# A convolution and a low-rank mixer on one core: two h clusters a slot in place of three, and the conv at other pieces of W2

## The chip, the cores and the metric

The kernel runs on one core of a Trainium2 chip. The metric is the time of one execution on the device in microseconds (us): the median of 3 runs was 324.3 us (324.24 to 325.69). One further execution was profiled. It took 324.34 us, and the span from its first to its last instruction was 322.4 us. All times below are in us unless another unit stands there.

## The reference

The input `x` has 8 batches of 4224 rows (positions) with 192 columns. A causal convolution of 7 taps, with softmax weights for each of 8 heads of 24 columns, gives `y`. Then a mixer adds a low-rank product along the positions, and a two-layer network along the columns:

```python
y   = lightweight_conv(x, softmax(weight))        # 7 taps back, 8 heads of 24 columns
tt  = U.T @ y                                     # per batch: 32 x 192, the "sums"
u   = y + V.T @ tt                                # the second term is "h"
out = u + relu(u @ w_ch1) @ w_ch2                 # 192 -> 768 -> 192
```

The output is float32, 8 x 4224 x 192.

## The kernel before, in words

Positions are cut into tiles of 128: 33 tiles a batch (`NT`), 264 in all, and 33 groups of 8 tiles (`NG`, `GT`) that run across the borders of the batches. Tiles are counted through, so batch b has tiles 33b to 33b + 32, and group g has 8g to 8g + 7.

The steps of the work, and the engine of each:

- **conv** (`conv32`, lines 331 to 363): for two or three heads, 8 small matmuls a head (L349, 64 rows by 32 columns of the array) fill two banks of PSUM, and each bank is copied to `y_sb` by ScalarE ("A") or VectorE ("D"), as a pattern such as `AAD` says, taken in turn. Half of the matmuls read `xb_sb`, a shifted copy of `x_sb` that GpSimd makes (`x_shift`, lines 296 to 327).
- **sums** (`tt_mm`, `tt_split`, `tt_sum`): 33 matmuls (L412) make U.T y in four column groups; ScalarE takes `tt_hi` (L426), VectorE takes `tt_lo` (L427); later two matmuls (L438) add the four groups up, and VectorE writes `tt_sb` (L432). h needs `tt_sb` of its batch.
- **h** (`h_tiles`, lines 458 to 498): a matmul for each tile (L469, 32 rows of the array, so that four row groups can run at once; row group = pair number modulo 4). Two tiles of a batch, an even one and the next, share a PSUM bank. In a call, all even tiles are issued, and then all odd ones. VectorE adds `y_sb` and writes `u_sb` (L492), one add for a bank, or two where the bank's two tiles lie in different halves of four tiles.
- **transposes** (`transp`): a DMA on SP's queue turns a group's `u_sb` into `uT`.
- **W1** (`w1`): 36 matmuls a group (L587, 64 rows by 128 columns, two at once); relu to `rl_sb` on ScalarE (L601) or VectorE (L603), 7 and 5 a group.
- **W2** (`w2`): two tiles are a piece, with 12 matmuls on the whole array (L614), one bank, an add on VectorE (L623) and a transfer to the output on SP's queue.

All matmul results pass through one pool of eight PSUM banks, which are given out in turn (`bank()`); a bank is handed on when its last reader has finished.

The order is written by hand. A list `SLOTS` (lines 650 to 702) has for each slot the groups whose W1 runs first, the groups whose W2 then runs piece by piece, and a table `at`: before piece p of the slot, do these other steps. From slot 5 on a slot has three groups, so 12 pieces. Names in the table: `c5:0:2:A` is conv of batch 5, from head 0, two heads, copies on ScalarE; `x6:4` four of the six shifting steps of batch 6; `t5` and `s5` the two halves of the sums; `h16` is h of group 16 with its transpose. Slots 6 to 9 do conv and sums of batches 4 to 7 beside W2; slots 10 to 13 have no conv left. Loads of `x` are issued on GpSimd's queue during W1 (`LOADS`, `x_load`), and two of the six shifting steps go between them. Pools with few buffers: `xs` 2, `xbs` 1, `ys` 3, `us` 7, `uts` 5.

Of the kernel before, what the change touches and what calls it, by code (L numbers as in the profile page):

```python
# [14 lines left out]
def kernel(  # L15
# [12 lines left out]
    B, S, D = x.shape  # L28
# [7 lines left out]
    GT = 8  # L36
    NTT = B * NT
    NG = NTT // GT
# [292 lines left out]
    def conv32(b, h0, nh, engs):  # L331


        if yt[b] is None:
            yt[b] = ys.tile([P, NT, D], BF16, name="y_sb")
        nk = (NB0 // 2, NB1 // 2)
        for n in range(nh):
            h = h0 + n
            hs = slice(h * GS, h * GS + GS)
            pp = [bank(), bank()]  # L340
            for cg in range(4):
                t, w, st = (
                    (xt[b], bands[h // HQ][:, h % HQ, QB : 2 * QB], 1 + cg // 2)
                    if cg % 2
                    else (xbt[b], band2[:, h, :], cg // 2)
                )
                for r in range(2):
                    hr = slice(HB * r, HB * r + HB)
                    nc.tensor.matmul(  # L349
                        out=pp[r][QB * cg : QB * cg + QB, 0 : nk[r] * GS],  # L350
                        lhsT=w[hr],
                        rhs=t[hr, st : st + 2 * nk[r] - 1 : 2, hs],
                        start=True,
                        stop=True,
                        tile_position=(HB * r, QB * cg),
                    )
            for part in range(2):
                j0 = NB0 // 2 * part
                evac(
                    engs[(2 * n + part) % len(engs)],  # L360
                    yt[b][:, j0 : j0 + nk[part], hs],
                    pp[part][:, 0 : nk[part] * GS].rearrange("p (k a) -> p k a", a=GS),
                )
# [42 lines left out]
    def tt_mm(b, js, p=None):  # L406

        if p is None:
            p = bank()
        for n, j in enumerate(js):  # L410
            c = n % 4
            nc.tensor.matmul(  # L412
                out=p[32 * c : 32 * c + 32, 0:D],
                lhsT=U_sb[:, j // 4, j % 4, :],
                rhs=yt[b][:, j, :],
                start=(n < 4),
                stop=(n + 4 >= len(js)),
                tile_position=(0, 32 * c),
            )
        return p  # L420

    def tt_split(b, p):

        hi = sml.tile([P, D], BF16, name="tt_hi")
        lo = sml.tile([P, D], BF16, name="tt_lo")
        nc.scalar.activation(out=hi[:], in_=p[:, 0:D], func=ACT.Copy)  # L426
        nc.vector.tensor_tensor(out=lo[:], in0=p[:, 0:D], in1=hi[:], op=ALU.subtract)  # L427
        ttb[b] += [hi, lo]
# [29 lines left out]
    def h_tiles(b, j0, j1):  # L458

        banks = {}  # L460
        for a in range(2):
            for pr in range(j0 // 2, (j1 + 1) // 2):
                j = 2 * pr + a
                if not j0 <= j < j1:
                    continue
                q = pr % 4
                if pr not in banks:
                    banks[pr] = bank()
                last = nc.tensor.matmul(  # L469
                    out=banks[pr][:, a * D : (a + 1) * D],  # L470
                    lhsT=V_sb[32 * q : 32 * q + 32, (j // 8) * 2 + j % 2, :],
                    rhs=ttb[b][32 * q : 32 * q + 32, :],
                    start=True,
                    stop=True,
                    tile_position=(32 * q, 0),
                )
        done.append(last)
        for pr in sorted(banks):
            js = [j for j in (2 * pr, 2 * pr + 1) if j0 <= j < j1]
            runs = []  # L480
            for j in js:
                t = b * NT + j
                if runs and t % 4 != 0:
                    runs[-1].append(j)
                else:
                    runs.append([j])
            for run in runs:
                n = len(run)
                t = b * NT + run[0]
                g, hf, i = t // GT, (t % GT) // 4, t % 4  # L490
                a = run[0] % 2
                nc.vector.tensor_tensor(  # L492
                    out=u_group(g)[:, i : i + n, :, hf, :],
                    in0=yt[b][:, run[0] : run[0] + n, :].rearrange("p n (c k) -> p n c k", c=3),
                    in1=banks[pr][:, a * D : (a + n) * D].rearrange(
                        "p (n c k) -> p n c k", n=n, c=3
                    ),
                    op=ALU.add,
                )

    def h_group(g):
        t0, t1 = g * GT, g * GT + GT
        while t0 < t1:
            b = t0 // NT
            te = min(t1, (b + 1) * NT)
            h_tiles(b, t0 - b * NT, te - b * NT)
            t0 = te

    def transp(g):
        uTt[g] = uts.tile([P, 4, 3, P], BF16, name="uT")  # L510
        return nc.sync.dma_start_transpose(
            out=uTt[g][:].rearrange("p i c t -> p (i c) t"),
            in_=ut[g][:].rearrange("p i c f k -> p (i c f k)"),
        )
# [118 lines left out]
    def held(ins, after):  # L633
        tc.add_manual_dep(
            ins.ins,
            after.ins.name,
            mybir.DependencyInfo(mybir.DependencyClass.Sync, mybir.DependencyReason.DATA),
            reason="transfer held back",
        )

    def x_load(b, q, after):
        if q == 0:
            x_tile(b)
            x_zero(b, nc.gpsimd)
        held(x_part(b, *XP[q]), after)
# [4 lines left out]
    SLOTS = [  # L650
        ([0], [], {}),
        ([1], [0], {0: ["h0", "l2:0", "l2:1"], 1: ["h3", "l2:2"]}),
        (
            [2],
            [1],
            {0: ["d1", "x2:1", "l2:3", "x2:5", "h1"], 1: ["t1"], 3: ["s1"], 4: ["h4"]},
        ),
        ([3], [2], {1: ["h5"], 3: ["h6"]}),
# [12 lines left out]
            },  # L671
        ),
    ]
    nh = 10
    for k in range(5, 14):
        gs = list(range(3 * k - 9, 3 * k - 6))
        hs = [f"h{g}" for g in range(nh, min(nh + 3, NG))] + [None] * 3
        nh = min(nh + 3, NG)
        if k == 5:
            at = {  # L680
                2: ["c3:0:3:AAD"],
                3: ["c3:3:3:AAD"],
                4: ["c3:6:2:A", "x4:4"],
                5: [hs[0]],
                6: ["t3"],
                8: ["s3", hs[1]],
                11: [hs[2]],
            }
        elif k < 10:
            b = k - 2  # L690
            at = {
                0: [f"c{b}:0:2:A"],
                2: [f"c{b}:2:3:AAD"],
                3: [f"c{b}:5:3:AAD"] + ([f"x{b + 1}:4"] if b + 1 < B else []),
                5: [f"t{b}", hs[0]],
                7: [f"s{b}"],
                8: [hs[1]],
                11: [hs[2]],
            }
        else:  # L700
            at = {0: [hs[0]], 4: [hs[1]], 8: [hs[2]]}
        SLOTS.append((gs, gs, {p: [w for w in what if w] for p, what in at.items()}))
    assert nh == NG

    LOADS = {3: [(4, 1), (4, 4), (5, 1), (5, 4)]}
    for b in range(4, B):
        g = 3 * b - 6
# [83 lines left out]
    def do(what):  # L791
        if what[0] == "c":
            b, h0, n, engs = what[1:].split(":")
            conv32(int(b), int(h0), int(n), engs)
            return
        if what[0] == "d":
            for h in range(H):
                last = conv(int(what[1:]), h, 1, [0, 1], "AA" if h == 2 else "AD")
            held(transp(3), last)
            done.append(last)  # L800
            return
        if what[0] == "l":
            b, q = (int(v) for v in what[1:].split(":"))
            x_load(b, q, done[-1])
            return
        if what[0] == "x":
            b, n = (int(v) for v in what[1:].split(":"))
            if not steps:
                steps.extend(x_shift(b))
            for _ in range(n):  # L810
                steps.pop(0)()
            return
        n = int(what[1:])
        if what[0] == "h":
            h_group(n)
            if n > 1 and n != 3:
                transp(n)
        elif what[0] == "t":
            tt_split(n, tt_mm(n, range(NT)))
        else:  # L820
            tt_sum(n)

    for gs1, gs2, at in SLOTS:
# [13 lines left out]
        for p in range(npc + 1):  # L837
            for what in at.get(p, []):
                do(what)
            if p < npc:  # L840
                g, k = gs2[p // 4], p % 4
# [35 lines left out]
```

## Time and profile before

| quantity | value |
|---|---|
| median of 3 runs | 324.3 us |
| profiled execution: time, span | 324.34 us, 322.4 us |
| granted TensorE clock | 1.00 |
| TensorE busy with matmuls | 316.4 us, 98% |
| VectorE, ScalarE, GpSimd busy | 268.9, 169.6, 141.8 us |
| W2 (L614) | 1584 matmuls |
| W1 (L587) | 1188 matmuls |
| h (L469) | 264 matmuls, 168 adds on VectorE (L492) |
| conv (L349), from batch 2 on | 384 matmuls |

How to read it: the profile's page has busy times, a chain that ended last (followed back from the last instruction), and groups of instructions. The same chain can be shown in order of time, as pieces "start, duration, engine and line, how many instructions". A timeline of one engine has for each run of instructions the start, the duration, the operation, out<-in with shapes, and in brackets the idle time ahead of it and what ended it. Matmuls are pipelined: a row's duration is longer than the distance to the next row, so what a matmul costs is read from starts. The same holds for VectorE: durations overlap by some 0.08 us.

### The profile page before, as it was taken

Reading aid. Unit: us, or ns where it says so; the run is one execution under the profiler, and the core shown is the slowest. Engines: PE = TensorE matmul, PEld = TensorE weight load, DVE = VectorE, ACT = ScalarE, POOL = GpSimd, SP = SyncE. Lnnn points to the kernel's source line nnn. Section 1 sums busy time; section 2 is a strip of 40 time slices with the busy share of each in tenths; the row PEclk is TensorE's granted clock in tenths of the full one; section 3 lists DMA queues with packets and bytes.
Section 4 is the critical chain, followed back from the end, with each engine's and each line's share of the span. In section 5 each row is a group of like instructions: output and inputs, shape, how many; then the busy total and the mean of one; then the engine's idle time right before and its main releaser. Section 6 shows DMA issues by size and latency. Waiting matters only on the chain.

```text
span 322.4 us, 9590 instructions
## 1 busy us (share of the span) xinstructions
PE 316.4 (98%) x4004; PEld 223.3 (69%) x4004; DVE 268.9 (83%) x550; ACT 169.6 (53%) x344; POOL 141.8 (44%) x108
## 2 busy tenths in 40 slices
PE   8999999999999999999999999999999999999996
PEld 3757576478678647867864884687797497487495
DVE  6769989987977986997898699789888897896864
ACT  1766723960874397088249609824903902912910
POOL 8763299429937983992897497000000000000000
PEclk9999999999999999999999999999999999999999
DMA  8999994999997999799689966138269059039035
GB/s 103 191 195 169 200 226 104 213 179 243 190 188 142 266 151 191 151 185 190 170 230 187 188 171 173 51 107 232 59 177 264 3 148 292 5 97 291 7 121 174
DMA packets 122442, 53.38 MB, mean 166 GB/s; under 512 B 87712, under 2 KB 122400, under 8 KB 122400
## 3 DMA queue, kind: packets, MB, share of 16 engines
q1 hardware_dynamic: 84528, 38.08, 47.4%
q0 software_dynamic: 37728, 14.60, 39.3%
q8 instruction: 31, 0.51, 0.7%
q10 hardware_dynamic: 144, 0.10, 0.1%
q14 instruction: 11, 0.09, 0.1%
HBM read 29.22 MB, written 25.95 MB: 171 GB/s over the span
## 4 chain that ended last, share of the span: by engine, by line
PE 91%; ACT 4%; DMA 2%; DVE 2%; issue 1%; POOL 0%; POOLq 0%
PE ps L614 42%; PE ps L587 39%; PE ps L349 3%; PE ps L469 3%; DMA x_sb<-in_x_dram 2%; PE ps L412 2%; ACT rl_sb L601 2%; ACT y_sb L266 2%; PE ps L379 1%; DVE u_sb L492 1%; DVE rl_sb L603 1%; PE ps L438 0%; PE ps L534 0%; POOL x_sb L79 0%; DVE out_sb L623 0%
## 5 line engine op out<-in xcount | busy, mean ns | idle before, releaser
L601 ACT ACTIVATE rl_sb<-ps 128x512 bf16<-128x512 f32 x233 | 124.3, 604 | 107.7 <-PE ps L587 95.7
L614 PE MATMUL ps<-W_sb,rl_sb 128*128 128x192 bf16 x1584 | 141.2, 246 | 0.2
L614 PEld LDWEIGHTS <-rl_sb 128*128 128x128 bf16 x1584 | 128.3, 98 | 11.8 <-issue 11.4
L587 PE MATMUL ps<-uT,W_sb 64*128 64x512 bf16 x1188 | 131.7, 376 | 0.3 <-DVE uT L268 0.2
L603 DVE TENSOR_SCALAR rl_sb<-ps 128x512 bf16<-128x512 f32 x163 | 105.3, 687 | 14.9 <-PE ps L587 14.7
L587 PEld LDWEIGHTS <-W_sb 64*128 64x128 bf16 x1188 | 66.8, 94 | 60.7 <-issue 4.0
L623 DVE TENSOR_TENSOR out_sb<-ps,u_sb 128x384 f32<-128x384 f32 (+1 forms) x133 | 70.3, 549 | 25.5 <-PE ps L614 25.0
L315 POOL COPY xb_sb<-x_sb 32x3072 bf16<-32x3072 bf16 (+1 forms) x24 | 67.7, 2822 | 1.1
L492 DVE TENSOR_TENSOR u_sb<-y_sb,ps 128x192 bf16<-128x192 bf16 (+1 forms) x168 | 66.2, 460 | 0.0
L303 POOL COPY xb_sb<-x_sb 128x3072 bf16<-128x3072 bf16 x12 | 32.9, 2744 | 39.5 <-PE ps L349 32.4
L266 ACT ACTIVATE y_sb<-ps 128x384 bf16<-128x384 f32 (+4 forms) x90 | 38.3, 519 | 9.8 <-PE ps L349 7.4
L79 POOL DMA_DIRECT2D x_sb<-in_x_dram x32 | 27.1, 853 | 13.9 <-PE ps L469 7.7
L268 DVE CAST y_sb<-ps 128x408 bf16<-128x408 f32 (+4 forms) x36 | 19.1, 577 | 1.4 <-PE ps L379 1.3
L469 PE MATMUL ps<-tt_sb,V_sb 32*128 32x192 bf16 x264 | 12.4, 246 | 0.1
L349 PE MATMUL ps<-x_sb,band 64*32 64x384 bf16 x192 | 12.1, 333 | 0.0
L349 PE MATMUL ps<-xb_sb,band 64*32 64x384 bf16 x192 | 12.1, 332 | 0.0
L469 PEld LDWEIGHTS <-V_sb 32*128 32x128 bf16 x264 | 4.7, 92 | 7.3 <-issue 7.3
L426 ACT ACTIVATE tt_hi<-ps 128x192 bf16<-128x192 f32 x8 | 2.6, 331 | 11.9 <-PE ps L412 11.9
L379 PE MATMUL ps<-x_sb,band 64*64 64x240 bf16 (+3 forms) x192 | 7.9, 275 | 0.5 <-DMA x_sb<-in_x_dram 0.4
L349 PEld LDWEIGHTS <-band 64*32 64x32 bf16 x384 | 4.5, 89 | 5.2 <-issue 2.4
L163 PE MATMUL ps<-zz 128*128 128x512 f32 (+1 forms) x10 | 6.5, 804 | 1.1 <-DVE zz L151 1.1
L379 PEld LDWEIGHTS <-band 64*64 64x64 bf16 x192 | 6.0, 106 | 2.2 <-issue 1.6
(65 smaller groups left out, 67.9 us busy)
## 6 DMA issues: line engine op xcount, KB each, us to landing
out_dram<-out_sb SPq DMA_DIRECT2D x131, 192.0 KB, 2.7
x_sb<-in_x_dram POOLq DMA_DIRECT2D x14, 384.0 KB, 7.6
x_sb<-in_x_dram POOLq DMA_DIRECT2D x7, 432.0 KB, 8.3
x_sb<-in_x_dram POOLq DMA_DIRECT2D x7, 408.0 KB, 7.8
W_sb<-in_moe_w_ch_dram POOLq DMA_DIRECT2D x3, 288.0 KB, 7.5
x_sb<-in_x_dram POOLq DMA_DIRECT2D x1, 504.0 KB, 7.5
uT<-u_sb SPq DMA_TRANSPOSE x31, 4.2
x_sb<-in_x_dram POOLq DMA_DIRECT2D x1, 480.0 KB, 5.7
```

Of the source, the lines that this page charges most:

```text
L79: return nc.gpsimd.dma_start(out=xt[b][HB * r : HB * r + HB, s0:s1, :], in_=x[b, blk * HB : (blk + s1 - s0) * HB, :].rearrange("(j p) d -> ...
L266: nc.scalar.activation(out=out, in_=in_, func=ACT.Copy)
L303: nc.gpsimd.tensor_copy(out=xbt[b][:, s0:s1, :], in_=xt[b][:, s0 + 1 : s1 + 1, :])
L315: nc.gpsimd.tensor_copy(out=xbt[b][q, s0:s1, :], in_=xt[b][q, s0:s1, :])
L349: nc.tensor.matmul(out=pp[r][QB * cg : QB * cg + QB, 0 : nk[r] * GS], lhsT=w[hr], rhs=t[hr, st : st + 2 * nk[r] - 1 : 2, hs], start=True, ...
L469: last = nc.tensor.matmul(out=banks[pr][:, a * D : (a + 1) * D], lhsT=V_sb[32 * q : 32 * q + 32, (j // 8) * 2 + j % 2, :], rhs=ttb[b][32 * ...
L492: nc.vector.tensor_tensor(out=u_group(g)[:, i : i + n, :, hf, :], in0=yt[b][:, run[0] : run[0] + n, :].rearrange("p n (c k) -> p n c k", c=3),
L587: last = nc.tensor.matmul(out=pps[m][hf][:], lhsT=W1_sb[HB * hf : HB * hf + HB, c, m * P : (m + 1) * P], rhs=uTt[g][HB * hf : HB * hf + HB ...
L601: nc.scalar.activation(out=rl[:, m, hf, :], in_=pp[hf][:], func=ACT.Relu)
L603: nc.vector.tensor_scalar_max(out=rl[:, m, hf, :], in0=pp[hf][:], scalar1=0.0)
L614: last = nc.tensor.matmul(out=cps[:, a * D : (a + 1) * D], lhsT=rlt[g][:, m, hf, (i + a) * P : (i + a + 1) * P], rhs=W2_sb[:, m, :], start ...
L623: nc.vector.tensor_tensor(out=o[:, 0:n, :].rearrange("p n (c k) -> p n c k", c=3), in0=cps[:, 0 : n * D].rearrange("p (n c k) -> p n c k", ...
```

## The change

From slot 5 on h is no longer done by groups of 8 tiles but by spans of tiles (`w105:117` and so on): slot 5 has 8, 8 and 9 tiles, slots 6 to 11 have two spans of 11 or 12, slot 12 has 8 and 11. Each span ends at the end of a PSUM bank (an odd tile number within the batch, or the last tile of a batch). After a span, the transposes of all groups that it completes are issued. In slots 6 to 9, conv stands before pieces 0, 2 and 4 in place of 0, 2 and 3, with other patterns of copying engines (`AAD`, `A`, `AD` in place of `A`, `AAD`, `AAD`); h stands before pieces 5 and 9 in place of 5, 8 and 11; the sums begin before piece 9 in place of 5, and end after piece 11 in place of before piece 7. In slots 10 and 11 h stands before pieces 2 and 7, in slot 12 before 0 and 5 (before: 0, 4, 8).

```diff
+    def h_span(t0, t1):
         while t0 < t1:
             b = t0 // NT
             te = min(t1, (b + 1) * NT)
             h_tiles(b, t0 - b * NT, te - b * NT)
             t0 = te
+
+    def h_group(g):
+        h_span(g * GT, g * GT + GT)
...
-    nh = 10
+    spans = {
+        5: [(80, 88), (88, 96), (96, 105)],
+        6: [(105, 117), (117, 129)],
+        7: [(129, 140), (140, 152)],
+        8: [(152, 164), (164, 175)],
+        9: [(175, 187), (187, 198)],
+        10: [(198, 210), (210, 222)],
+        11: [(222, 233), (233, 245)],
+        12: [(245, 253), (253, 264)],
+        13: [],
+    }
     for k in range(5, 14):
         gs = list(range(3 * k - 9, 3 * k - 6))
-        hs = [f"h{g}" for g in range(nh, min(nh + 3, NG))] + [None] * 3
-        nh = min(nh + 3, NG)
+        hs = [f"w{t0}:{t1}" for t0, t1 in spans[k]]
...
         elif k < 10:
             b = k - 2
             at = {
-                0: [f"c{b}:0:2:A"],
-                2: [f"c{b}:2:3:AAD"],
-                3: [f"c{b}:5:3:AAD"] + ([f"x{b + 1}:4"] if b + 1 < B else []),
-                5: [f"t{b}", hs[0]],
-                7: [f"s{b}"],
-                8: [hs[1]],
-                11: [hs[2]],
+                0: [f"c{b}:0:2:AAD"],
+                2: [f"c{b}:2:3:A"],
+                4: [f"c{b}:5:3:AD"] + ([f"x{b + 1}:4"] if b + 1 < B else []),
+                5: [hs[0]],
+                9: [f"t{b}", hs[1]],
+                12: [f"s{b}"],
             }
+        elif k < 13:
+            at = {0 if k == 12 else 2: [hs[0]], 5 if k == 12 else 7: [hs[1]]}
         else:
-            at = {0: [hs[0]], 4: [hs[1]], 8: [hs[2]]}
...
+        if what[0] == "w":
+            t0, t1 = (int(v) for v in what[1:].split(":"))
+            h_span(t0, t1)
+            for g in range(t0 // GT, t1 // GT):
+                transp(g)
+            return
```

More of the change, by code (lines that the diff above doesn't have):

```diff
@@ L499, in h_tiles @@
                 )
-    def h_group(g):
-        t0, t1 = g * GT, g * GT + GT
+    def h_span(t0, t1):
         while t0 < t1:
@@ L691 @@
             at = {
-                0: [f"c{b}:0:2:A"],
-                2: [f"c{b}:2:3:AAD"],
-                3: [f"c{b}:5:3:AAD"] + ([f"x{b + 1}:4"] if b + 1 < B else []),
-                5: [f"t{b}", hs[0]],
-                7: [f"s{b}"],
-                8: [hs[1]],
-                11: [hs[2]],
-            }
-        else:
-            at = {0: [hs[0]], 4: [hs[1]], 8: [hs[2]]}
-        SLOTS.append((gs, gs, {p: [w for w in what if w] for p, what in at.items()}))
-    assert nh == NG
+                0: [f"c{b}:0:2:AAD"],
[4 more added lines that the diff above has]
+                12: [f"s{b}"],
+            }
+        elif k < 13:
+            at = {0 if k == 12 else 2: [hs[0]], 5 if k == 12 else 7: [hs[1]]}
+        else:
+            at = {}
+        SLOTS.append((gs, gs, at))
     LOADS = {3: [(4, 1), (4, 4), (5, 1), (5, 4)]}
```

## The prediction

> **What bounds the kernel now.** I read the page's busy times, then its chain, then the chain in order of time over slots 6 and 7, then VectorE's timeline over the same stretch.
>
> ```profile
> PE 316.4 (98%) x4004; PEld 223.3 (69%) x4004; DVE 268.9 (83%) x550; ACT 169.6 (53%) x344; POOL 141.8 (44%) x108
> PE 91%; ACT 4%; DMA 2%; DVE 2%; issue 1%; POOL 0%; POOLq 0%
> ```
>
> TensorE bounds it: 98% busy, 91% of the chain, and from 67 us on the chain hardly leaves it. Its granted clock is 1.00 throughout, so matmul rows can be added and subtracted. The chain by pieces:
>
> ```profile
> 136.84 11.91 PE ps L587 x108
> 148.75 0.47 PE ps L349 x11
> 149.22 2.09 PE ps L614 x24
> 151.31 0.64 PE ps L349 x19
> 151.95 1.10 PE ps L614 x12
> 153.05 0.71 PE ps L349 x17
> 153.76 2.09 PE ps L614 x24
> 155.84 0.85 PE ps L412 x33
> 156.69 0.35 PE ps L469 x8
> 157.04 2.09 PE ps L614 x24
> 159.13 0.17 PE ps L438 x2
> 159.29 0.99 PE ps L614 x12
> 160.28 0.28 PE ps L469 x8
> 160.56 3.08 PE ps L614 x36
> 163.64 0.28 PE ps L469 x8
> 163.91 1.10 PE ps L614 x12
> 165.01 11.76 PE ps L587 x108
> ```
>
> This is slot 7 complete: W1 of three groups (11.91), then W2 with conv (L349), the sums (L412, L438) and three clusters of h (L469); 165.01 opens slot 8. Three prices are in it. A W2 piece (12 matmuls) is 0.99, and a run of W2 that ends in front of smaller tiles pays 0.11 more (1.10, 2.09, 3.08 are one, two, three pieces plus 0.11). A cluster of 8 h tiles is 0.28; where it crosses from one batch to the next it is 0.35. Eight h matmuls run as two rounds of four row groups; the crossing makes a third round, so a round is some 0.08 and the fixed part of a cluster 0.28 - 0.16 = 0.12. A third conv of 24 matmuls is 0.71 where the second is 0.64: a wait of 0.07 for banks.
>
> ```profile
> 136.30 2.06 DVE L492 TENSOR_TENSOR u_sb<-y_sb,ps 128x192 bf16<-128x192 bf16 x6
> 138.29 0.55 DVE L623 TENSOR_TENSOR out_sb<-ps,u_sb 128x384 f32<-128x384 f32 x1
> 138.75 4.26 DVE L603 TENSOR_SCALAR rl_sb<-ps 128x512 bf16<-128x512 f32 x7
> 157.09 0.36 DVE L427 TENSOR_TENSOR tt_lo<-ps,tt_hi 128x192 bf16<-128x192 f32 x1 [0.65 <-ACT tt_hi L426]
> 160.95 1.94 DVE L492 TENSOR_TENSOR u_sb<-y_sb,ps 128x384 bf16<-128x384 bf16 x4
> ```
>
> VectorE is the second limit. At the end of slot 6 it still works off h when W1 is on TensorE: its first relu is at 138.75, 1.91 after W1 began, and that W1 took 11.91, not 11.76. After slot 9 the lag was 1.83 and W1 11.83; after slot 8 it was 1.63 and W1 11.76. So a lag up to about 1.75 is free, and beyond it TensorE pays. Back to back, an add over a whole bank comes every 0.465 (next row at 162.80), half a bank every 0.265 (138.29 - 136.30 = 1.99 for two whole and four halves), an output add every 0.467.
>
> **The change part by part.** Times in a slot are from T = 0 at its first conv matmul; all in us.
>
> *Switches and h on TensorE.* Slots 6 to 9 now have five W2 runs that end before smaller tiles (before the second conv, the third, the first h, the sums, W1), not six: -0.11 a slot. A cluster of 11 or 12 tiles fills six banks. Its pairs take the row groups in turn, all first tiles and then all second ones, so the order is like 0 1 2 3 0 1, 0 1 2 3 0 1. A row group can't start its next matmul before its last, which makes four rounds, not three: 0.12 + 4 x 0.08 = 0.44; with a crossing from batch 4 to 5 (tiles 164 to 174) or 6 to 7 (222 to 232) five, 0.52. No row shows a 12-tile cluster: from below it is 0.36 (three full rounds), from above 0.52; I take 0.44, because the crossing rows show that a repeated row group does cost a round. Before, h was 0.84 in slot 6 and 0.91 or 0.92 in 7 to 9; after, 0.88, 0.88, 0.96, 0.88. With the switch: -0.07, -0.14, -0.07, -0.15, together -0.43. So merging clusters saves a fixed 0.12 and gives 0.16 back in rounds; the gain is the switch.
>
> *Slots 10 to 12.* Before 0.84, 1.01 (0.45 + 0.28 + 0.28) and 0.75 (0.47 + 0.28); the 0.45 and 0.47 hold a wait for a bank straight after W1 or a crossing. After: 0.88, 0.96, 0.72. The exits are equal in number. Together -0.04, taken as 0.
>
> *Adds and banks on VectorE.* Counted over tiles 80 to 263, both kernels make 65 adds over a whole bank and 54 over half. No VectorE work goes away; 107 banks become 95. In place of 8 tiles after pieces 5, 8 and 11 of W2, VectorE gets 12 after pieces 5 and 9. One cluster costs it 6 x 0.465 = 2.79, in a stretch with odd offsets 3 x 0.465 + 6 x 0.265 = 2.99.
>
> *Does TensorE wait at the second cluster?* This decides. There are eight banks in turn. Slot 6, the worst (odd offsets): the relu tail ends at 0.8; conv casts on VectorE are one after the first conv and three after the third (before: two and two, equal in total). The third conv starts at 5.28; its casts run 5.88 to 7.38, the output add of piece 4 to 7.85, the first h (TensorE at 7.02 to 7.46) to 10.83, then four output adds to 12.70. TensorE runs pieces 5 to 8 to 11.54, the sums to 12.37, and the second h at once. Its fourth to sixth banks are those of pieces 5 to 7, free by 12.3; piece 9 starts at 12.81 in the bank of piece 8, free at about 12.8. That is no slack at all in slot 6, and hardly more in slot 9 (its first cluster is as dear); with 2.59 or 2.79 for the first cluster, slots 7 and 8 have 0.4 and 0.2. Ends: from below 0, from above 0.4 a slot (six banks take 2.8 to empty, the cluster and two free banks cover 0.44 + 1.98). I take 0.1 in slots 6 and 9, +0.2, nearest to the sum above.
>
> *What waits behind it.* tt_lo needs tt_hi from ScalarE; VectorE stood 0.65 for that (157.09). Now it is still busy with the adds then (hi is done at 12.81, VectorE free at 12.70), so 0.1. That idle time pays for the later h. Behind tt_lo: the second h to 16.10, three output adds to 17.50, tt_sb to 17.77, while W1 starts at about 16.1. The lag is 1.7, under 1.75: the 0.15 and 0.07 of W1 go, -0.22. Between -0.22 and +0.2 (a lag of 2.0). The new sums' second half (0.17) stands before W1 and is no longer between pieces: same price.
>
> *Slot 5.* Its last cluster has nine tiles, three rounds as before; one half add becomes a whole one, +0.2 on VectorE: a lag of 1.55 becomes 1.75, +0.05.
>
> *Conv.* First conv: three of its four casts on ScalarE, one on VectorE, where VectorE waited 0.87 for work. The second has all six on ScalarE: 2.98 to 5.55 at 0.41 apart; the third needs its last bank at about 5.65. Its wait is between 0 and 0.14, before 0.07: no change.
>
> *Queues.* SP issues the same transposes and output transfers; one or two transposes follow a cluster. Slot 7's group 17 is transposed at about T + 14.5; with 1.44 to issue and 4.2 to land it is there at 20.1, and its W1 is at 16.1 + 7.84 = 23.9. POOL's copies of x start when the third conv is over, 5.9 and not 5.0; the last one ended at 145.38 for a conv at 148.75, so 3.3 of slack become 2.3. Both cost nothing.
>
> Sum: -0.43 + 0.2 - 0.22 + 0.05 = -0.4 on the profiled execution, 324.34 with a span of 322.4, which is 0.01% off the median of 324.3. Forecast **323.9**.
>
> A rule that speaks against the change is in the Trainium skill, "TensorEngine Tiling (Array Packing)", section PSUM Bottleneck: tiling makes TensorE faster but not the emptying of PSUM, so the copy may become the limit. Taken strictly, every one of some 13 six-bank clusters would cost the 0.4 above, and the time would by estimate be about 329. The rows speak for less: banks come free one at a time, and the next W2 piece needs one only every 0.99, against 0.465 for an add.
>
> **The rivals.**
> *Slower: VectorE is late at the second cluster.* For it: no slack in slots 6 and 9, and 83% busy. Against: a lag is paid once, since TensorE's wait lets VectorE catch up, and its idle time falls from 2.8 to about 2.4 a slot. Each 0.1 of lateness costs 0.1 in that slot. It decides from 0.5 a slot over four slots (+2.0 - 0.4 = +1.6), with a full loss also of W1: 325.9 to 326.5. Chance 0.12.
> *Faster: h runs in three rounds.* Then 0.36 a cluster, -0.08 x 13 = -1.0 more, and with the third conv's 0.07 gone in four slots -0.3: 322.6. Against: the 0.35 rows. Chance 0.08.
> *Transposes land late.* The longest landing shown is 9.1, with 2.3 to issue: 25.9 against 23.9, 2.0 in up to three slots, 326 or more. For it: two in a row, and one group less of lead. Against: the median 4.2. Chance 0.02.
> *Nothing happens on the chain.* What the switch saves is lost in the wait of the second cluster: 324.3. Inside the forecast's own range.
>
> **How the numbers follow.** 0.5% (1.6) is about what a measurement of this kernel can tell from no change: its runs went from 324.24 to 325.69. Within it 0.78, faster 0.08, slower 0.12 + 0.02 = 0.14. The range goes down to -0.43 - 0.22 - 0.6 (half of the three-round gain): 322.8, and up to the 0.4 a slot of waiting in four slots, with the runs' own spread: 326.0.
>
> **What would show it.** Right: two h groups a slot of some 0.44, five exits of 0.11, W1 at 11.76 in every slot, slots 6 to 9 some 0.1 shorter each. Wrong: L614 at the second cluster with gaps, longer than 0.99 a piece, ended by VectorE's adds; a 12-tile cluster at 0.36 or over 0.6; W1 over 11.9.

## The result, and the profile after

The changed kernel takes 323.38 us (median of 12 executions, 323.08 to 324.20), the kernel before 324.87 us (12, 324.21 to 326.07). The ratio is 0.9955 with a 95% interval of 0.9943 to 0.9967: 0.45% faster, just inside the 0.5% that the prediction called no change. The forecast was 323.9 with a range of 322.8 to 326.0. The executions of the kernel before lie in two groups, six at 324.21 to 324.65 and six at 325.08 to 326.07, and their median falls in the gap; of the changed kernel's twelve, eleven lie at 323.08 to 323.60. The profiled execution took 323.12 us, with a span of 321.3 us against 322.4.

The page of the changed kernel, busy times and the chain by engine:

```profile
PE 314.9 (98%) x4004; PEld 218.7 (68%) x4004; DVE 268.7 (84%) x550; ACT 169.5 (53%) x344; POOL 141.6 (44%) x108
...
PE 91%; ACT 3%; DMA 2%; DVE 2%; POOL 1%; issue 1%; POOLq 0%
```

TensorE still bounds it, and did 1.5 less of busy time; VectorE did the same work. The chain in order of time (start, duration, engine and line, instructions), slot 7 complete, with W1 of slot 8 as its last line:

```profile
136.62 11.76 PE ps L589 x108
148.38 0.47 PE ps L349 x11
148.85 2.09 PE ps L616 x24
150.93 0.64 PE ps L349 x19
151.57 2.09 PE ps L616 x24
153.66 0.64 PE ps L349 x19
154.30 1.09 PE ps L616 x12
155.40 0.43 PE ps L469 x11
155.83 4.07 PE ps L616 x48
159.90 0.85 PE ps L412 x33
160.74 0.43 PE ps L469 x12
161.18 3.08 PE ps L616 x36
164.25 0.17 PE ps L438 x2
164.42 11.76 PE ps L589 x108
```

(L616 is W2, L589 is W1; the lines moved by two.) W1 at the top took 11.91 before. From the first conv to W1 this slot takes 164.42 - 148.38 = 16.04, where it took 165.01 - 148.75 = 16.26. Both clusters of 11 and 12 tiles are 0.43. All conv blocks of 24 are 0.64. No piece holds a wait. VectorE's timeline at the end of slot 6, first its `tt_lo` before, then the rows after:

```profile
129.00 0.36 DVE L427 TENSOR_TENSOR tt_lo<-ps,tt_hi 128x192 bf16<-128x192 f32 x1 [0.65 <-ACT tt_hi L426]
```

```profile
131.28 1.95 DVE L625 TENSOR_TENSOR out_sb<-ps,u_sb 128x384 f32<-128x384 f32 x4
133.34 0.36 DVE L427 TENSOR_TENSOR tt_lo<-ps,tt_hi 128x192 bf16<-128x192 f32 x1
133.61 3.06 DVE L492 TENSOR_TENSOR u_sb<-y_sb,ps 128x384 bf16<-128x384 bf16 x9
...
138.25 4.41 DVE L605 TENSOR_SCALAR rl_sb<-ps 128x512 bf16<-128x512 f32 x7
```

The four output adds of pieces 5 to 8 end at 133.23, and tt_lo follows almost at once: in slots 6 and 9 the 0.65 of standing still before it are gone. In slots 7 and 8, whose first cluster has fewer half adds, 0.51 and 0.31 are left. The first relu comes at 138.25. W1 began at 136.62 in the chain, so VectorE's lag is 1.63 where it was 1.91.

Where the 1.1 of the span went, by pieces of the chain, is an account of four terms. (Sums here and below are made of unrounded starts and can differ by 0.01 from those of the rows. An exit is a run of W2 that ends in front of smaller tiles.)

| term | before to after | sum |
|---|---|---|
| h, and one exit of W2 less, slots 6 to 9 | 0.28/0.35 three times to 0.43 or 0.51 twice, six exits to five | -0.42 |
| third conv, slots 6 to 9 | 0.71 to 0.64 | -0.27 |
| W1 after slots 6 and 9 | 11.91 and 11.83 to 11.76 | -0.22 |
| slots 10 to 12 | 13.03, 13.20, 12.84 to 13.07, 13.15, 12.80 | -0.05 |

Together -0.96, from the first conv of slot 6 to the start of the last W1: 295.46 - 120.67 = 174.79 before, 294.40 - 120.57 = 173.83 after. Another 0.1 lies in the time before slot 6.

### The profile page after: what moved, and what is told of

It reads as the page before. It is cut to its first block, busy times and chain, and to the rows that moved or that the text cites. A ratio compares the mean times of both kernels' runs of the same rounds, so it can differ in the third digit from the quotient of the medians.

```text
span 321.3 us, 9597 instructions
## 1 busy us (share of the span) xinstructions
PE 314.9 (98%) x4004; PEld 218.7 (68%) x4004; DVE 268.7 (84%) x550; ACT 169.5 (53%) x344; POOL 141.6 (44%) x108
## 4 chain that ended last, share of the span: by engine, by line
PE 91%; ACT 3%; DMA 2%; DVE 2%; POOL 1%; issue 1%; POOLq 0%
PE ps L616 42%; PE ps L589 39%; PE ps L349 3%; PE ps L469 3%; DMA x_sb<-in_x_dram 2%; PE ps L412 2%; ACT rl_sb L603 2%; ACT y_sb L266 1%; PE ps L379 1%; POOL x_sb L79 1%; DVE u_sb L492 1%; DVE rl_sb L605 1%; PE ps L438 0%; PE ps L536 0%; DVE out_sb L625 0%
## 5 line engine op out<-in xcount | busy, mean ns | idle before, releaser
L616 PE MATMUL ps<-W_sb,rl_sb 128*128 128x192 bf16 x1584 | 139.8, 246 | 0.2
L616 PEld LDWEIGHTS <-rl_sb 128*128 128x128 bf16 x1584 | 128.4, 98 | 12.2 <-issue 11.9
L589 PE MATMUL ps<-uT,W_sb 64*128 64x512 bf16 x1188 | 131.5, 376 | 0.3 <-DVE uT L268 0.2
L589 PEld LDWEIGHTS <-W_sb 64*128 64x128 bf16 x1188 | 61.3, 94 | 65.9 <-issue 3.0
L625 DVE TENSOR_TENSOR out_sb<-ps,u_sb 128x384 f32<-128x384 f32 (+1 forms) x133 | 69.5, 550 | 25.9 <-PE ps L616 25.0
L266 ACT ACTIVATE y_sb<-ps 128x408 bf16<-128x408 f32 (+4 forms) x90 | 38.2, 519 | 11.9 <-PE ps L349 9.8
L469 PEld LDWEIGHTS <-V_sb 32*128 32x128 bf16 x264 | 5.8, 92 | 5.7 <-issue 5.5
L412 PE MATMUL ps<-y_sb,U_sb 128*32 128x192 bf16 x258 | 7.4, 247 | 0.0
```

The source lines that it names most:

```text
L266: nc.scalar.activation(out=out, in_=in_, func=ACT.Copy)
L469: last = nc.tensor.matmul(out=banks[pr][:, a * D : (a + 1) * D], lhsT=V_sb[32 * q : 32 * q + 32, (j // 8) * 2 + j % 2, :], rhs=ttb[b][32 * ...
L589: last = nc.tensor.matmul(out=pps[m][hf][:], lhsT=W1_sb[HB * hf : HB * hf + HB, c, m * P : (m + 1) * P], rhs=uTt[g][HB * hf : HB * hf + HB ...
L616: last = nc.tensor.matmul(out=cps[:, a * D : (a + 1) * D], lhsT=rlt[g][:, m, hf, (i + a) * P : (i + a + 1) * P], rhs=W2_sb[:, m, :], start ...
L625: nc.vector.tensor_tensor(out=o[:, 0:n, :].rearrange("p n (c k) -> p n c k", c=3), in0=cps[:, 0 : n * D].rearrange("p (n c k) -> p n c k", ...
```

## The experiments

In the eleven profiles, the two kernels' and those of the nine experiments, everything ahead of slot 6 ended anywhere between 120.6 and 122.2 (the loads and the first transposes are never quite alike; in three profiles a W1 there waited 0.6 to 1.2 for a transpose), although the code there differs at most by one tile of h. From slot 6 on, pieces with the same neighbours repeat to 0.01. So beside the ratio I give the *stretch*: from the first conv of slot 6 to the start of the last W1, 174.79 before and 173.83 after. It shows effects of 0.1 that the ratio can't.

The change has three parts: in slots 6 to 9 conv at other pieces with other copying engines, in slots 5 to 12 h in clusters, and in slots 6 to 9 the sums later. All eight combinations were run. Diffs of a part alone are against the kernel before, all others against the changed kernel; they show the table `at` of slots 6 to 9.

### Conv alone

```diff
-                0: [f"c{b}:0:2:A"],
-                2: [f"c{b}:2:3:AAD"],
-                3: [f"c{b}:5:3:AAD"] + ([f"x{b + 1}:4"] if b + 1 < B else []),
+                0: [f"c{b}:0:2:AAD"],
+                2: [f"c{b}:2:3:A"],
+                4: [f"c{b}:5:3:AD"] + ([f"x{b + 1}:4"] if b + 1 < B else []),
                 5: [f"t{b}", hs[0]],
                 7: [f"s{b}"],
                 8: [hs[1]],
                 11: [hs[2]],        # hs: the three groups of 8 tiles
```

> Conv at pieces 0, 2, 4 with the new patterns of copying engines; h in three groups of 8 and the sums at pieces 5 and 7 as before. Theory (the gain is a sum of small terms of TensorE): only the third conv changes, 0.71 to 0.64 in four slots, so -0.3 us, ratio 0.999; h 0.28 or 0.35 and six exits of 0.11 a slot as before; W1 after slots 6 and 9 still 11.83 to 11.91. Rival (the placing of conv brings all of it, the clusters nothing): -1.1 us or more, ratio 0.9955 to 0.9965, W1 11.76 in every slot.

Measured: ratio 1.0002 (0.9988 to 1.0016), stretch 174.94, +0.15. The third conv did go to 0.64. But the sums begin one piece after it, and its copies are not done. The chain, then VectorE's casts of the same place:

```profile
126.31 0.64 PE ps L349 x19
126.95 1.10 PE ps L616 x12
128.05 0.95 PE ps L412 x33
```

```profile
126.82 1.55 DVE L268 CAST y_sb<-ps 128x408 bf16<-128x408 f32 x3
```

The casts end at 128.37, the sums wanted to start at 128.05, and take 0.95, not 0.85. So 0.07 won and 0.10 lost in each slot. Both theories missed: the rival by far, mine by this wait. W1 stays at 11.91 after slot 6, as I expected.

### Clusters alone

```diff
                 0: [f"c{b}:0:2:A"],
                 2: [f"c{b}:2:3:AAD"],
                 3: [f"c{b}:5:3:AAD"] + ([f"x{b + 1}:4"] if b + 1 < B else []),
                 5: [f"t{b}", hs[0]],     # hs: two spans of 11 or 12 tiles
                 7: [f"s{b}"],
-                8: [hs[1]],
-                11: [hs[2]],
+                9: [hs[1]],
```

> h in two clusters at pieces 5 and 9 (later slots as in the changed kernel); conv as before at 0, 2, 3 with its old patterns, sums at 5 and 7 as before. Theory: one exit of 0.11 less in four slots and some 0.05 in h in all, -0.5 us, ratio 0.9985; the third conv stays at 0.71; VectorE still stands some 0.65 for tt_hi, so its lag at W1 stays near 1.9 and W1 after slot 6 stays at about 11.9. Rival (merging gives back in rounds what it saves): 0.0 us, ratio 1.000.

Measured: ratio 1.0022 (1.0003 to 1.0040), stretch 175.05, +0.26: slower. (The ratio is some 0.7 us, more than the stretch: the rest is not in it. In this profile slot 6 begins at 122.24, in that of before at 120.67.) TensorE's timeline at the second cluster of slot 6:

```profile
132.71 2.14 PE L616 MATMUL ps<-W_sb,rl_sb 128*128 128x192 bf16 x24
134.78 0.78 PE L469 MATMUL ps<-tt_sb,V_sb 32*128 32x192 bf16 x12
135.63 0.57 PE L616 MATMUL ps<-W_sb,rl_sb 128*128 128x192 bf16 x5
```

From 134.78 to 135.63 the cluster takes 0.85 in place of 0.43. The chain leaves TensorE there, and goes back to the start of the first cluster (`...` stands for rows between):

```profile
129.34 0.86 PE ps L412 x33
...
130.22 0.34 ACT tt_hi L426
...
130.58 0.22 DVE tt_lo L427
...
130.86 0.96 DVE u_sb L492 x3
...
131.85 1.12 DVE u_sb L492 x4
...
134.30 0.55 DVE out_sb L625
...
135.11 0.48 DVE out_sb L625
...
135.63 3.13 PE ps L616 x36
```

VectorE stands still for tt_hi until 130.58, and then has six banks to empty in one go, the output adds behind them; four pieces of W2 are not long enough. This is the rival "VectorE is late at the second cluster" of the prediction, in a kernel that does not have the later sums. In slot 7 the second cluster takes its 0.43 and waits for nothing. Both expectations, -0.5 and 0.0, missed by this wait; and W1 is 11.76 everywhere, not 11.9 after slot 6.

### Sums alone

```diff
-                5: [f"t{b}", hs[0]],
-                7: [f"s{b}"],
+                5: [hs[0]],
                 8: [hs[1]],
-                11: [hs[2]],
+                11: [f"t{b}", hs[2]],
+                12: [f"s{b}"],
```

> All as before, but the sums begin with the third h group at piece 11 and end after piece 11. Theory: TensorE has the same pieces and exits; VectorE's lag at W1 goes from 1.9 to about 1.7, W1 11.76 in slots 7 and 10, -0.2 us, ratio 0.9995. Rival 1 (the late sums are the gain): -1 us, ratio 0.997. Rival 2 (the second half of the sums waits for tt_lo right before W1): a gap before L438 of 0.3 or more in four slots, +1.2 us, ratio 1.004.

Measured: ratio 1.0011 (0.9993 to 1.0029), stretch 174.67, -0.12. TensorE's pieces are those of before; W1 after slots 6 to 9 is 11.80, 11.76, 11.80, 11.76: in sum -0.14 where -0.2 was expected, since after slot 8 it is 0.04 longer than before. No gap before L438. The theory holds in kind, and both rivals fall.

### Two parts at a time

Clusters and conv, with the sums as before:

```diff
                 4: [f"c{b}:5:3:AD"] + ([f"x{b + 1}:4"] if b + 1 < B else []),
-                5: [hs[0]],
-                9: [f"t{b}", hs[1]],
-                12: [f"s{b}"],
+                5: [f"t{b}", hs[0]],
+                7: [f"s{b}"],
+                9: [hs[1]],
```

> Conv and clusters as in the changed kernel, the second cluster at 9, but the sums at 5 and 7 as before. Theory (TensorE's savings count only where VectorE and ScalarE have emptied the banks in time; it is the move of the sums that gives them the time): the sums start 0.95 in place of 0.85 (copies of the third conv late, as with conv alone), the W2 pieces before and after the second cluster wait some 0.5 in slots 6 and 9 and 0.1 to 0.2 in 7 and 8, third conv 0.64; from the first conv of slot 6 to the end +0.4 to +0.7 on before (201.8), ratio 1.002. Rival (two of three parts bring two thirds of the gain): -0.6, ratio 0.998.

Measured: ratio 1.0011 (0.9997 to 1.0024), stretch 175.21, +0.42. The sums take 0.97 in the chain, the second cluster in slot 6 0.85: both waits of the single edits are there. The theory holds at the low end of its +0.4 to +0.7, and the rival's -0.6 falls.

Clusters and sums, with conv as before:

```diff
-                0: [f"c{b}:0:2:AAD"],
-                2: [f"c{b}:2:3:A"],
-                4: [f"c{b}:5:3:AD"] + ([f"x{b + 1}:4"] if b + 1 < B else []),
+                0: [f"c{b}:0:2:A"],
+                2: [f"c{b}:2:3:AAD"],
+                3: [f"c{b}:5:3:AAD"] + ([f"x{b + 1}:4"] if b + 1 < B else []),
```

> Clusters and sums as in the changed kernel (before pieces 5, 9 and after 11), conv as before at 0, 2, 3 with the old patterns. Theory: no bank wait at the second cluster, one exit less, W1 11.76 in every slot, third conv stays at 0.71: -0.6 to -0.75 from the first conv of slot 6 to the end, ratio 0.998. Rival (the parts add up: +0.48 for clusters alone, -0.12 for the sums alone): +0.36, ratio 1.001.

Measured: ratio 0.9986 (0.9971 to 1.0001), stretch 174.10, -0.69. The chain of slot 6:

```profile
125.15 0.71 PE ps L349 x17
125.86 2.09 PE ps L616 x24
127.95 0.44 PE ps L469 x12
128.38 4.07 PE ps L616 x48
132.45 0.85 PE ps L412 x33
133.30 0.44 PE ps L469 x12
133.73 3.08 PE ps L616 x36
```

The same cluster that took 0.85 is 0.44 here: four pieces of W2 and the sums (0.85) lie between the clusters, and no tt_lo stands in front of the first. The parts do not add up: +0.26 and -0.12 alone make -0.69 together, as the theory had it (-0.6 to -0.75).

Conv and sums, with three groups of 8:

```diff
                 5: [hs[0]],         # hs: the three groups of 8 tiles
-                9: [f"t{b}", hs[1]],
+                8: [hs[1]],
+                11: [f"t{b}", hs[2]],
                 12: [f"s{b}"],
```

> Conv as in the changed kernel, h in three groups of 8 before 5, 8, 11, the sums with the third group and after piece 11. Theory: third conv 0.64 in four slots, no wait at the sums, W1 11.76 to 11.80: -0.4 to -0.5 from the first conv of slot 6 to the end, ratio 0.9985. Rival (the parts add up: +0.16 for conv alone, -0.12 for the sums alone): +0.04, ratio 1.000.

Measured: ratio 0.9973 (0.9958 to 0.9988), stretch 174.40, -0.39. Third conv 0.64, sums 0.85, W1 11.76 to 11.80. That is the theory, at the low end of its -0.4 to -0.5, and not the sum of the parts.

| stretch against before | sums early | sums late |
|---|---|---|
| neither | 0 | -0.12 |
| conv | +0.15 | -0.39 |
| clusters | +0.26 | -0.69 |
| both | +0.42 | -0.96 |

With the sums early each of the other edits loses; with the sums late each wins, and then they add up nearly: -0.12 - 0.27 - 0.57 = -0.96.

### The copying engines

```diff
-                0: [f"c{b}:0:2:AAD"],
-                2: [f"c{b}:2:3:A"],
-                4: [f"c{b}:5:3:AD"] + ([f"x{b + 1}:4"] if b + 1 < B else []),
+                0: [f"c{b}:0:2:A"],
+                2: [f"c{b}:2:3:AAD"],
+                4: [f"c{b}:5:3:AAD"] + ([f"x{b + 1}:4"] if b + 1 < B else []),
```

> The changed kernel with conv at 0, 2, 4 but the old patterns A, AAD, AAD of copying engines. Theory: two pieces of W2 between the convs are enough for the copies whichever engine makes them, third conv 0.64, time as the changed kernel, ratio 0.9955. Rival (the split of the copies between the engines is needed): third conv at 0.71 or the first cluster delayed by 0.1 or more, +0.3 to +0.6 us on the changed kernel, ratio 0.997.

Measured: ratio 1.0014 (1.0001 to 1.0028), stretch 175.01, +1.18 on the changed kernel. The third conv is 0.64 as expected, but the time is not that of the changed kernel: my theory fell. The rival had the right wait, at the first cluster, and half its size. The chain in slot 6:

```profile
127.01 0.36 PE ps L349 x5
127.37 1.68 ACT y_sb L266 x4
...
129.09 0.40 PE ps L469 x7
```

With `AAD` the third conv has four of its six copies on ScalarE, some 0.41 apart. They end at 129.05; the first cluster follows one piece later, needs six banks, and waits: W2 phases are longer by 0.31, 0.23, 0.31, 0.32. With `AD` it is three and three, and nothing waits.

### The second cluster earlier

```diff
-                9: [f"t{b}", hs[1]],
+                8: [f"t{b}", hs[1]],
```

> The changed kernel with the sums and the second h cluster one piece earlier, before piece 8. Theory (the second cluster waits for banks unless VectorE has emptied pieces 5 to 8; at piece 9 there is no slack in slots 6 and 9): its last banks and the bank of the next W2 piece are late by some 0.45 in slots 6 and 9, 0.1 to 0.25 in 7 and 8, so +1.3 us on the changed kernel, ratio to before 0.9995. Rival (banks do not bind there): the time of the changed kernel, ratio 0.9955.

Measured: ratio 0.9999 (0.9986 to 1.0011), stretch 175.08, +1.25 on the changed kernel; by slots +0.48, +0.08, +0.20, +0.48. The theory gave 0.45 in slots 6 and 9, 0.1 to 0.25 in 7 and 8, 1.3 in all, and the rival nothing. TensorE in slot 6:

```profile
132.25 0.86 PE L469 MATMUL ps<-tt_sb,V_sb 32*128 32x192 bf16 x12
133.18 3.05 PE L616 MATMUL ps<-W_sb,rl_sb 128*128 128x192 bf16 x35
```

0.93 for a cluster of 0.43. So the bank count of the prediction is shown: at piece 8 it is half a microsecond too early, at piece 9 just in time.

### The second cluster later

```diff
-                9: [f"t{b}", hs[1]],
+                11: [f"t{b}", hs[1]],
```

> The changed kernel with the sums and the second h cluster at piece 11. Theory (a lag of VectorE at the start of W1 over 1.75 is paid one for one): lag 2.8 to 3.0 in four slots, W1 12.8 to 13.0 in place of 11.76, +4 to +5 us on the changed kernel, ratio 1.009 to 1.011. Rival (VectorE catches up within W1, whose relus leave it idle some 1.2 a W1): W1 below 12.0, under +1 us, ratio below 0.999.

Measured: ratio 1.0042 (1.0027 to 1.0057), stretch 176.48, +2.65 on the changed kernel. VectorE in slot 6, where W1's first matmul starts at 136.53:

```profile
135.31 0.36 DVE L427 TENSOR_TENSOR tt_lo<-ps,tt_hi 128x192 bf16<-128x192 f32 x1 [0.65 <-ACT tt_hi L426]
135.58 3.06 DVE L492 TENSOR_TENSOR u_sb<-y_sb,ps 128x384 bf16<-128x384 bf16 x9
...
139.29 1.27 DVE L605 TENSOR_SCALAR rl_sb<-ps 128x512 bf16<-128x512 f32 x2
```

The 0.65 of standing still are back, and the lag is 2.76 from that matmul. W1 took 12.59, 12.45, 12.26 and 12.39 for lags of 2.76, 2.56, 2.41 and 2.56. Less 11.76 that is 0.83, 0.69, 0.50, 0.63: what is over some 1.9 is paid about one for one. From the same mark, before had 1.98 (0.15 paid) and 1.90 (0.07), the changed kernel at most 1.85 and nothing. The expectation had the mechanism right and the sum too large: it took the lag at 2.8 to 3.0, and it is 2.4 to 2.8. The rival, under +1, falls.

## Why the prediction was right, and where its sizes were off

The forecast of 323.9 and its range held; the gain was -0.96 in the stretch and some -1.1 in the profiled span, where -0.4 was forecast. What it called the gain is there: one exit less and a shorter W1, with four rounds a cluster. It had less than half of the size, because what it added for the second cluster and slot 5 did not come, and conv and slots 10 to 12, taken as nothing, gained; these errors all point the same way and none cancels another. Step by step:

- *Switches and h.* Forecast -0.43, measured -0.42. The four rounds of a cluster were taken at 0.44 and are 0.43, the five rounds at 0.52 and are 0.51. The row that decided it, a crossing group at 0.35, carried over. The rival of three rounds (0.36) fell.
- *W1.* Forecast -0.22, measured -0.22; the lag after slot 6 was forecast at 1.7 and is 1.63.
- *The second cluster.* +0.2 was taken, 0 was measured. The sum had slot 6 with no slack, the last add at 12.70 and the next piece at 12.81, and was right in that (12.66 and 12.81 after the start of the slot): the adds end at 133.23, the cluster starts at 132.94 and the next piece at 133.38, both without a gap. I rounded the missing slack up to a price. The earlier cluster shows how sharp the edge is, and the slower rival is what happens without the later sums (+0.26 and +0.42).
- *Conv.* Taken as no change, with a wait between 0 and 0.14; measured no wait at all, -0.27. This is the largest term that was mis-sized. Two pieces of W2 between the second and the third conv give ScalarE the time for six copies in a row. My sum had the last one end at 5.55, and the third conv in need of its bank at about 5.65. The row in slot 6 ends at 125.94, 5.37 after the start of the slot:

```profile
123.48 2.46 ACT L266 ACTIVATE y_sb<-ps 128x384 bf16<-128x384 f32 x6 [1.07 <-PE ps L349]
```

- *Slot 5.* +0.05 was taken, and W1 after it is 11.76 as before: 0. *Slots 10 to 12* were -0.04 by the rows and taken as 0; -0.05 was measured.
- *Queues.* No W1 from slot 6 on waits for a transpose. GpSimd's last copy in slot 6 ends at 146.00 for a conv at 148.38, 2.4 of slack where 2.3 was forecast.
- *The range.* Its lower end was written as 322.8, but the terms named for it, -0.43 - 0.22 - 0.6, are -1.25, which is 323.1. The measured 323.38 lies above that too.
- *The rule on emptying PSUM.* The Trainium skill, "TensorEngine Tiling (Array Packing)", section PSUM Bottleneck, says that tiling makes TensorE faster but not the emptying of PSUM, so that the copy may become the limit. The estimate of about 329 was for a wait at every cluster; here none waits. The rule is seen at work at the second cluster in the kernels with the clusters and the early sums, and with the second cluster at piece 8 (0.42 to 0.49 in slot 6), and at the first cluster in the kernel with the old patterns (0.23 to 0.32 a slot), there by ScalarE's copies.

What stays open: the interval of the ratio, -0.33% to -0.57%, is -1.1 to -1.9, and the stretch with -0.96 lies at its small end or just outside. Part of this is the spread of the kernel before. Its lower group has a median of 324.40, which is 1.0 above the changed kernel's 323.38 and fits the stretch; and beside the experiments, in 20 to 35 executions each, its median was 324.47 to 324.49, 1.1 above. So about 0.3% is the gain that the traces account for, and the 0.45% has the rest from how many executions before fell into the upper group, 6 of 12. Why so many did, and one of 12 after, no run here settles: the edit ahead of slot 6 is one tile, and the time to slot 6 differs by up to 1.7 between the profiles.

## What to carry to other kernels

On a saturated engine, price a reordering by its switches (here the exits) and fixed parts first, and then walk the buffers (here eight PSUM banks) in the order in which they are given out: each gain holds only if the engine that empties them gets there in time, and that engine's own standing still (VectorE for tt_hi) can be put where it is busy anyway. Edits that share such a resource need not add up (here +0.15, +0.26 and -0.12 alone make -0.96 together); test them in combinations before one of them is thrown away, since two of these three lose time when they are made alone. Where a sum comes out at exactly no slack, the price is nought or a step, and the neighbouring placement shows which side it is on.

## What the runs showed of the hardware that was not expected

- A run of W2 in front of smaller tiles costs 0.11 more than whole pieces (1.10, 2.09, 3.08, 4.07, 5.06 for one to five), and the price did not depend on how long the run was, 12 to 84 matmuls. A cluster of h fits 0.12 plus 0.08 a round, where a row group that comes again opens a new round: 0.28, 0.35, 0.43 and 0.51 for two to five.
- W1's tolerance for a late VectorE is sharp: a lag up to 1.85 costs nothing, 1.90 and 1.98 cost 0.07 and 0.15, and of 2.41 to 2.76 all above some 1.9 is paid, although VectorE then stands still for 0.49 and 0.60 later in the same W1.
- Pieces with the same neighbours from slot 6 on repeat to 0.01 between the eleven profiled executions, while the first 120 us differ by up to 1.7 with nearly the same code.
